# Two pieces instead of three for the turned maxima, queued reciprocals, and a re-ordered last stretch in an attention and token-mixer kernel

## The chip, the cores and the metric

The kernel runs on one core of one Trainium2 chip. The metric is the device time of one execution in microseconds (us). Before the change three runs took 1679.13 to 1680.25 us, with a median of 1679.38 us. The profiled execution is one more run: 1679.48 us, of which the profile covers a span of 1677.7 us.

## The reference

The input x has 2048 tokens of 512 channels. Two branches read its normalised rows. Cut to what matters:

```python
xn = layernorm(x)
# A: softmax attention, 32 heads of 16 channels
q, k, v = split(xn @ wqkv)
o = softmax(q @ k.T * 16 ** -0.5) @ v          # per head, 2048 x 2048 scores
s = o @ wo
# B: an MLP over the token axis, F = 1792
h = layernorm(xn)
u = gelu(einsum("bsd,sf->bdf", h, w1) + b1)
y = einsum("bdf,fs->bds", u, w2) + b2
out = x + s * silu(y.transpose())
```

All is float32. Products are made from values split into an upper part and a remainder (`three`: three matmuls for one product).

## The kernel before, in words

**The order is written out by hand.** The program is a list of instructions that each engine works off in its own order; no scheduler moves anything. Python loops over steps `s` in twos ("a pair"), from 0 to `total` = 534. `NU` = 512 is the number of half-blocks of maxima; `LEAD` = 22 is how many steps the maxima run ahead of the scores.

**One pair of the long middle part** (steps 22 to 510) holds, for two heads that sit in the two halves of TensorE's rows:

- 8 matmuls `mx` (line 393) of scores whose row maximum alone is wanted. VectorE reduces each one from PSUM (line 397, `mxp`). The pool `ps_mx` has three banks, so the fourth `mx` waits for the first reduction.
- 8 matmuls `sc` (line 771) of the scores that are used; ScalarE takes their exponentials (line 776, `prob`).
- two bursts of values, `values` (line 787, `av`), each of four matmuls that accumulate numerator and denominator of the softmax.
- up to 12 half matmuls of the token mixer (line 938, `dn`).

The strings in `ORDERS`, `ENDS` and `BEGINS` set the order of these within a pair, and the two numbers behind them (`places`) say in front of which entry the two bursts stand. At each place `piece()` is called, then the burst, then `run_later()`, which runs work that was put off by `after(n, f)` for n such calls.

**The maxima's sets.** After every 8 pairs, 16 half-blocks of maxima are complete (`max_rows`). They are reduced once more and negated on VectorE (line 412, `neg`), turned in four 32 x 32 blocks by VectorE (line 409, `f`), split by GpSimd (line 420, `m`) and written by four DMAs of GpSimd's queue as two extra rows of q. So the later score matmul subtracts the maximum by itself. `max_rows` returns these steps as functions; they go to the list `pieces`, and `piece()` runs one of them. There are 32 sets, 30 of them with both places of their pair in the middle part.

**Reciprocals.** For each group `g` of heads and each half `span` of the queries, `invert` takes the reciprocal of the denominators `d` (line 555, VectorE) and stores them (`rec_d`). There are eight. `divisions` later loads them and multiplies; `divide` puts its product on GpSimd while `now[0] < NU` and on VectorE afterwards (`eng`). The last of the six-head groups, span 1, gates the sixteen blocks of output products in `rest` (`until`).

**The last part.** From step 512 no maxima are left: a pair is 8 scores, two bursts and two calls of `take`, each of which takes one block of output products (line 897), as far as one is allowed. `own` handles the last pair of heads without a round trip through memory: turn with TensorE (`one`, line 629), reciprocal (632), a copy that spreads it (633), turn back (`two`, line 641), then `chunk`: multiply (647), upper part on ScalarE (648), remainder (79). For span 0 this runs between scores. For span 1 it runs at the very end, in four chunks of 128 columns, and 24 last matmuls (lines 86 to 88), eight multiplications by the gate (1093), eight additions (1097; four on GpSimd, four on VectorE) and eight stores follow.

Of the kernel before, what the change touches and what calls it, by code (L numbers as in the profile page):

```python
# [21 lines left out]
def tile_attention_token_mixer(ctx, tc, x, wqkv, wo, w1, b1, w2, b2, out):  # L22
    nc = tc.nc
    P = 128
# [339 lines left out]
    el = pool("el", 2, reuse_waits="tile")  # L364

    later = []
    now = [0]
# [31 lines left out]
    def max_rows(u):  # L399
# [17 lines left out]
        def last():  # L417
            turned(3)
            m = sm.tile([16, 2, P], F32R, name="m", bufs=1)
# [9 lines left out]

        return first_, lambda: turned(1, 2), last  # L430

# [117 lines left out]
    def invert(g, span):  # L549

        n = heads_of(g)
        d = dens[span][: DH * n, :]

        def two():
            nc.vector.reciprocal(d, d)
            nc.sync.dma_start(rec_d[g][span][:n, :].rearrange("h (j q) -> (h j) q", j=16), d)
            away.add((g, span))

        after(8 if g < ND - 1 else 4, two)

# [59 lines left out]
    def own(span, ev):  # L620
        rq = sm.tile([P, 4, 4], F32, name="rq", bufs=1)
        wide = el.tile([P, 512], F32, name="t", bufs=4)

        def one(pl=ps_mx, nm="mx"):

# [5 lines left out]
            for a in range(2):  # L631
                nc.vector.reciprocal(rq[:, :, 2 * a : 2 * a + 2], turned[:, :, 2 * a : 2 * a + 2, 16 - 16 * a])
            nc.vector.tensor_copy(
                wide.rearrange("p (k j r) -> p k j r", k=4, j=4), rq.unsqueeze(3).to_broadcast([P, 4, 4, 32]),
            )

        def two(pl=ps_mx, nm="mx"):

            ps = pl.tile([P, 512], F32, name=nm)
            for k in range(4):  # L640
                nc.tensor.matmul(
# [3 lines left out]

        def chunk(ps, of, at):
            nc.vector.tensor_tensor(out=ev[:, at], in0=ps[:, at], in1=ev[:, at], op=OP.mult)
            nc.scalar.copy(of[:, 0, at], ev[:, at])
            sub(nc.vector, of[:, 1, at], ev[:, at], of[:, 0, at])

        if span == QH - 1:
            asides.extend((one, two, chunk))
            return

        def move_in():
            ps = two()
            of = el.tile([P, 2, 512], F32R, name="uo")
            chunk(ps, of, slice(0, 512))
            for a in range(2):
# [314 lines left out]
    first_maxima = []  # L974
    pieces = []

# [7 lines left out]
    for s in range(0, total + 1, 2):  # L984
# [9 lines left out]
        if s < NU and t >= 0:  # L994
# [7 lines left out]
            for i, kinds in enumerate((*zip(first, second), "")):  # L1002
                if i in places:

                    piece()
                    now[0] = s + places.index(i)
# [48 lines left out]
        if s < NU and s % 16 == 14:  # L1055
            pieces.extend(max_rows(s + 1))
        while t < 0 and piece():
# [13 lines left out]
    run_later()  # L1071
    one, two, chunk = asides
# [5 lines left out]
    for k in range(4):  # L1078
        chunk(ps, of, slice(k * P, (k + 1) * P))
# [5 lines left out]
    banks = [(ps_sc, "sc"), (ps_mx, "mx"), (ps_sc, "sc"), (ps_mx, "mx"), (ps_sc, "sc"), (ps_av, "av"), (ps_mx, "mx"), (ps_dn, "dn")]  # L1085
    half = [NB // 2 + 4 * c + k for k in range(4) for c in range(2)]
    for n, b in enumerate(half):
        pl, nm = banks[n]
        po = pl.tile([P, 512], F32, name=nm)[:, :D]
# [3 lines left out]
        nc.vector.tensor_tensor(out=gates[b], in0=po, in1=gates[b], op=OP.mult)  # L1093

    for eng, some in ((nc.gpsimd, half[:4]), (nc.vector, half[4:])):
        for b in some:
            eng.tensor_tensor(out=gates[b], in0=ys[b], in1=gates[b], op=OP.add)
            nc.sync.dma_start(out[b * P : (b + 1) * P, :], gates[b])

# [26 lines left out]
```

## Time and profile before

| what | us |
|---|---|
| median of three runs | 1679.38 |
| profiled execution | 1679.48 |
| its span | 1677.7 |
| TensorE busy | 1654.7 (99%) |
| VectorE busy | 1424.5 (85%) |
| ScalarE busy | 1200.3 (72%) |
| GpSimd busy | 574.8 (34%) |

The profile of the execution counts from the start of the span. PE is TensorE, PEld its weight loads, DVE is VectorE, ACT ScalarE, POOL GpSimd, and SPq the queue that issues most DMAs. Matmul ends are modelled, so a PE that is shown busy can still be late: whether it is held up is read from when a burst of values comes round again. In a timeline, each row has the start, the length, the engine, the line, the operation, `out<-in`, shapes and a count; in brackets stands how long the engine was idle before it, and what ended that.

### The profile page before, as it was taken

To read this page: it belongs to the slowest core of one execution; us is meant where nothing else is said; L and a number is where in the kernel's file an instruction comes from. 1 tells how busy PE (TensorE), PEld (TensorE's weight loads), DVE (VectorE), ACT (ScalarE), POOL (GpSimd) and SP (SyncE) were. 2 spreads that over 40 slices of the span, in tenths; PEclk is the share of its full clock that TensorE was granted. 3 is DMA by queue.
4 is the path that set the end of the run, shared out by engine and by line. 5 is a ranking of instruction groups with operands and counts; after the bars stand their busy time and mean duration, and the time that the engine had idled before them with its cause. 6 is when DMAs were issued, how large, how long until landed. Compare 5 with 4: busy or idle time off the path is not lost.

```text
span 1677.7 us, 30703 instructions
## 1 busy us (share of the span) xinstructions
PE 1654.7 (99%) x11700; PEld 870.6 (52%) x11700; DVE 1424.5 (85%) x2476; ACT 1200.3 (72%) x2295; POOL 574.8 (34%) x674
## 2 busy tenths in 40 slices
PE   7999999999999999999999999999999999999997
PEld 6887644554454545544454444455454444444443
DVE  6655988888988989889898989899898998899945
ACT  3333277777777777777877777777777778888874
POOL 3223853332344332342322322222223222642321
PEclk9999999999999999999999999999999999999999
DMA  6568621505132141916141613123142515363345
GB/s 213 186 233 201 120 73 46 88 24 92 40 67 65 46 64 37 246 55 106 35 83 33 100 49 49 52 53 67 35 69 62 84 36 93 118 125 101 116 144 197
DMA packets 152175, 155.30 MB, mean 93 GB/s; under 512 B 51596, under 2 KB 109964, under 8 KB 148956
## 3 DMA queue, kind: packets, MB, share of 16 engines
q1 hardware_dynamic: 147612, 152.59, 37.8%
q8 instruction: 92, 1.51, 0.4%
q0 software_dynamic: 4416, 0.75, 0.4%
q14 instruction: 55, 0.45, 0.1%
HBM read 101.86 MB, written 50.32 MB: 91 GB/s over the span
## 4 chain that ended last, share of the span: by engine, by line
PE 96%; DVE 1%; DMA 1%; ACT 0%; issue 0%; SPq 0%; POOL 0%; DVEq 0%; POOLq 0%
PE av L787 30%; PE dn L938 23%; PE mx L393 17%; PE sc L771 14%; PE dn L897 3%; PE mx L303 2%; PE sc L303 2%; DVE mxp L397 1%; PE av L897 1%; PE dn L303 1%; PE av L303 1%; PE sc L86 0%; PE sc L87 0%; PE sc L88 0%; PE mx L771 0%; DMA gt<-g_d 0%
## 5 line engine op out<-in xcount | busy, mean ns | idle before, releaser
L397 DVE TENSOR_REDUCE mxp<-mx 128x1 f32<-128x512 f32 x2004 | 1243.4, 682 | 147.8 <-PE mx L393 97.3
L776 ACT ACTIVATE prob<-sc 128x512 f32<-128x512 f32 x2004 | 1050.5, 603 | 300.1 <-PE sc L771 200.1
L771 PE MATMUL sc<-big 50*128 50x512 f32 x2004 | 756.0, 418 | 0.6
L393 PE MATMUL mx<-big 48*128 48x512 f32 x2004 | 744.5, 421 | 0.7
L787 PE MATMUL av<-prob,vp 128*32 128x512 f32 x4096 | 545.6, 605 | 0.0
L938 PE MATMUL dn<-hu,wh 64*128 64x512 f32 x1556 | 538.7, 406 | 0.0
L393 PEld LDWEIGHTS mx<-big 48*128 48x128 f32 x2004 | 358.6, 185 | 284.6 <-DVE mxp L397 261.9
L771 PEld LDWEIGHTS sc<-big 50*128 50x128 f32 x2004 | 358.5, 185 | 100.9 <-ACT prob L776 82.5
L938 PE MATMUL dn<-hu,wl 64*128 64x512 f32 x778 | 316.8, 407 | 0.0
L938 PEld LDWEIGHTS dn<-hu,wh 64*128 64x128 f32 x1556 | 284.4, 184 | 45.1 <-issue 23.8
L938 PEld LDWEIGHTS dn<-hu,wl 64*128 64x128 f32 x778 | 143.5, 184 | 107.5 <-issue 79.7
L787 PEld LDWEIGHTS av<-prob,vp 128*32 128x32 f32 x4096 | 80.9, 108 | 177.5 <-issue 166.3
L79 POOL TENSOR_TENSOR wl<-raw,wh 128x512 fp32r<-128x512 f32 x124 | 150.8, 1219 | 38.9 <-ACT wh L150 30.3
L148 POOL CAST wh<-raw 128x512 fp32r<-128x512 f32 (+1 forms) x107 | 62.3, 582 | 268.9 <-PE dn L938 171.7
L420 POOL CAST m<-f 16x128 fp32r<-16x128 f32 x32 | 9.0, 281 | 279.3 <-DVE f L409 279.3
L479 POOL TENSOR_TENSOR sq<-u 128x512 f32<-128x512 f32 x14 | 14.6, 1043 | 179.1 <-ACT u L478 179.1
L83 POOL DMA_DIRECT2D big<-m x128 | 68.0, 538 | 0.0
L938 PE MATMUL dn<-wh,hu 64*128 64x512 f32 x156 | 55.4, 408 | 0.0
L515 POOL TENSOR_SCALAR t<-t 128x512 f32<-128x512 f32 x16 | 23.9, 1491 | 80.0 <-ACT t L512 80.0
L79 POOL TENSOR_TENSOR hu<-hx,hu 128x512 fp32r<-128x512 f32 x16 | 20.4, 1294 | 57.1 <-ACT hu L246 57.1
L776 ACT ACTIVATE prob<-mx 128x512 f32<-128x512 f32 x44 | 27.3, 620 | 14.0 <-PE sc L771 8.8
L303 PE MATMUL mx<-xt,big 128*128 128x512 f32 x144 | 35.3, 394 | 0.0
(200 smaller groups left out, 1125.7 us busy)
## 6 DMA issues: line engine op xcount, KB each, us to landing
raw<-in_B_w_dram SPq DMA_DIRECT2D x104, 256.0 KB
big<-k_d SPq DMA_DIRECT2D x96, 128.0 KB
big<-q_d SPq DMA_DIRECT2D x96, 128.0 KB
q_d<-sg SPq DMA_DIRECT2D x16, 512.0 KB
k_d<-sg SPq DMA_DIRECT2D x16, 512.0 KB
num_d<-ev SPq DMA_DIRECT2D x30, 256.0 KB
u_d<-uo SPq DMA_DIRECT2D x14, 512.0 KB
hu<-u_d SPq DMA_DIRECT2D x14, 512.0 KB
```

The costliest lines, as they stand in the source:

```text
L79: eng.tensor_tensor(out=o, in0=a, in1=b.bitcast(F32), op=OP.subtract)
L83: queue.dma_start(dst.bitcast(F32), src.bitcast(F32))
L148: nc.gpsimd.tensor_copy(whs[n][:, :m, :], raws[n][:, :m, :])
L303: nc.tensor.matmul(ps, w[part][:, kd, m], xt[kd][:, z, :], start=w is wh and z == 0 and kd == 0, stop=w is wl and kd == ND - 1,)
L393: nc.tensor.matmul(ps, q[o : o + 48, r * P : (r + 1) * P], k[o : o + 48, c * 512 : (c + 1) * 512], start=True, stop=True,)
L397: nc.vector.tensor_reduce(mxp[u // 16][:, a, r % 8, c : c + 1], ps, axis=AX.X, op=OP.max)
L515: nc.gpsimd.tensor_scalar(t, t, 1.0, None, op0=OP.add)
L771: nc.tensor.matmul(ps, ks[p][o : o + 50, kb * P : (kb + 1) * P], qs[p][o : o + 50, at : at + 512], start=True, stop=True,)
L776: nc.scalar.activation(e, ps, AF.Exp, scale=scale)
L787: nc.tensor.matmul(av[32 * j : 32 * j + 32, :], vps[p][:, kb, 16 * a : 16 * a + 32], prob.pop((t, a, c)), start=kb == 0, stop=kb == NB - 1,)
L897: nc.tensor.matmul(ps, w(slice(0, P)), m(slice(0, P)), start=first, stop=last)
L938: made.append(lambda r=r, start=first and a == lead, stop=last and a != lead: nc.tensor.matmul(ps, w(r), m(r), start=start, stop=stop,))
```

## The change

1. `max_rows` returns two functions and not three: the second turns blocks 1, 2 and 3.
2. `piece()` is called at the first place of a pair only.
3. A reciprocal of `invert` is no longer run by `run_later`: when its time has come it goes to the end of `pieces`. A new set of maxima goes to the front of that list.
4. The last stretch: the copy that spreads the reciprocals is made in four parts, the turn back goes to four banks, `chunk` is cut into `times` and `lower` so that a remainder stands behind the next chunk's multiplication, matmuls are issued before any multiplication by the gate, banks are taken in another order, and GpSimd adds three blocks instead of four.

```diff
         def last():
-            turned(3)
+            turned(1, 2, 3)
...
-        return first_, lambda: turned(1, 2), last
+        return first_, last
...
-        after(8 if g < ND - 1 else 4, two)
+        after(8 if g < ND - 1 else 4, lambda: pieces.append(two))
...
-            nc.vector.tensor_copy(
-                wide.rearrange("p (k j r) -> p k j r", k=4, j=4), rq.unsqueeze(3).to_broadcast([P, 4, 4, 32]),
-            )
+            for k in range(0, 4, 4 // spread):
+                nc.vector.tensor_copy(
+                    wide.rearrange("p (k j r) -> p k j r", k=4, j=4)[:, k : k + 4 // spread],
+                    rq[:, k : k + 4 // spread].unsqueeze(3).to_broadcast([P, 4 // spread, 4, 32]),
+                )
...
-        def chunk(ps, of, at):
+        def times(ps, of, at):
             nc.vector.tensor_tensor(out=ev[:, at], in0=ps[:, at], in1=ev[:, at], op=OP.mult)
             nc.scalar.copy(of[:, 0, at], ev[:, at])
+
+        def lower(of, at):
             sub(nc.vector, of[:, 1, at], ev[:, at], of[:, 0, at])
...
-                    piece()
+                    if i == places[0]:
+                        piece()
...
-            pieces.extend(max_rows(s + 1))
+            pieces[:0] = max_rows(s + 1)
...
-    one(ps_sc, "sc")
+    one, two, times, lower = asides
+    one(ps_sc, "sc", 4)
     take(3, whole)
-    ps = two()
+    shares = [two(pl, nm, [k]) for k, (pl, nm) in enumerate([(ps_sc, "sc"), (ps_mx, "mx")] * 2)]
...
+    for k in range(5):
+        if k < 4:
+            times(shares[k], of, cols[k])
+        if k > 0:
+            lower(of, cols[k - 1])
+            for n in (2 * k - 2, 2 * k - 1):
+                product(n)
+
+    for n in range(8):
+        gated(n)
+        if n < 3:
+            added(n, nc.gpsimd)
+    for n in range(3, 8):
+        added(n, nc.vector)
```

What this does to the order on the engines is seen at three places. A row is a line, an operation, `out<-in` with the program's names, the size of the output and a count.

**VectorE, one set of maxima of the middle part with a reciprocal behind it.** `mxp` are the row maxima of one matmul, `neg_...` the set's negated maxima, `f` their turned form, `d` the denominators. Before:

```order
L412 TENSOR_REDUCE neg_130<-mxp 128x16
L409 STREAM_TRANSPOSE f<-neg_130 32x32
L397 TENSOR_REDUCE mxp<-mx 128x1 x3
L409 STREAM_TRANSPOSE f<-neg_130 32x32 x2
L397 TENSOR_REDUCE mxp<-mx 128x1 x5
L409 STREAM_TRANSPOSE f<-neg_130 32x32
L397 TENSOR_REDUCE mxp<-mx 128x1 x51
L555 RECIPROCAL d<-d 128x64
L397 TENSOR_REDUCE mxp<-mx 128x1 x5
```

After (the lines have moved: 409 is 410, 397 is 398, 412 is 413, 555 is 556):

```order
L413 TENSOR_REDUCE neg_130<-mxp 128x16
L410 STREAM_TRANSPOSE f<-neg_130 32x32
L398 TENSOR_REDUCE mxp<-mx 128x1 x8
L410 STREAM_TRANSPOSE f<-neg_130 32x32 x3
L398 TENSOR_REDUCE mxp<-mx 128x1 x8
L556 RECIPROCAL d<-d 128x64
L398 TENSOR_REDUCE mxp<-mx 128x1 x48
```

The two turns that stood after three reductions of the set's pair now stand one place further on, with the last one; a reciprocal no longer stands five reductions ahead of a set's end, but at the first place of the second pair behind a set.

**TensorE, the end of the wait for the last divided group, around step 512.** Matmuls of lines 771 and 777 are scores, 787 and 793 values, 897 and 903 the output products. Before:

```order
L787 MATMUL av<-prob,vp 32x512 x4
L771 MATMUL mx<-big 128x512
L771 MATMUL sc<-big 128x512
L771 MATMUL mx<-big 128x512
L771 MATMUL sc<-big 128x512
L771 MATMUL mx<-big 128x512
L771 MATMUL sc<-big 128x512
L787 MATMUL av<-prob,vp 32x512 x4
L897 MATMUL dn<-wh,hu 128x512
```

After, behind the same burst and the same six scores:

```order
L793 MATMUL av<-prob,vp 32x512 x4
L777 MATMUL mx<-big 128x512
L777 MATMUL sc<-big 128x512
L793 MATMUL av<-prob,vp 32x512 x4
L777 MATMUL mx<-big 128x512
L777 MATMUL sc<-big 128x512
L777 MATMUL mx<-big 128x512
L777 MATMUL sc<-big 128x512
L777 MATMUL mx<-big 128x512
L777 MATMUL sc<-big 128x512
L793 MATMUL av<-prob,vp 32x512 x4
L903 MATMUL dn<-wh,hu 128x512
```

One more pair goes by without output products, and all sixteen blocks come later by it. In exchange the half pair without one, which stood behind the seventh and eighth block (the wait for `own_done`), is gone, and so is one of the three at the end.

**VectorE, the last stretch.** `rq` are the reciprocals of the last pair of heads, `t` their spread form, `ev` numerators, `big` behind line 79 the remainder. Before:

```order
L633 COPY t<-rq 128x512
L647 TENSOR_TENSOR ev<-mx,ev 128x128
L79 TENSOR_TENSOR big<-ev,big 128x128
L647 TENSOR_TENSOR ev<-mx,ev 128x128
L79 TENSOR_TENSOR big<-ev,big 128x128
```

After:

```order
L635 COPY t<-rq 128x128 x4
L650 TENSOR_TENSOR ev<-sc,ev 128x128
L650 TENSOR_TENSOR ev<-mx,ev 128x128
L79 TENSOR_TENSOR big<-ev,big 128x128
L650 TENSOR_TENSOR ev<-sc,ev 128x128
L79 TENSOR_TENSOR big<-ev,big 128x128
```

The copy is in four parts, and each remainder stands behind the next multiplication. Behind these, on VectorE, stand eight multiplications by the gate as before, and then five additions in place of four.

More of the change, by code (lines that the diff above doesn't have):

```diff
@@ L364, in tile_attention_token_mixer @@
     el = pool("el", 2, reuse_waits="tile")
+    pieces = []
     later = []
@@ L622, in own, with one @@
         wide = el.tile([P, 512], F32, name="t", bufs=4)
-        def one(pl=ps_mx, nm="mx"):
+        def one(pl=ps_mx, nm="mx", spread=1):
             ps = pl.tile([P, 512], F32, name=nm)
@@ L632, in one, with two @@
                 nc.vector.reciprocal(rq[:, :, 2 * a : 2 * a + 2], turned[:, :, 2 * a : 2 * a + 2, 16 - 16 * a])
-            nc.vector.tensor_copy(
-                wide.rearrange("p (k j r) -> p k j r", k=4, j=4), rq.unsqueeze(3).to_broadcast([P, 4, 4, 32]),
-            )
-        def two(pl=ps_mx, nm="mx"):
+            for k in range(0, 4, 4 // spread):
[3 more added lines that the diff above has]
+                )
+        def two(pl=ps_mx, nm="mx", ks=range(4)):
             ps = pl.tile([P, 512], F32, name=nm)
-            for k in range(4):
+            for k in ks:
                 nc.tensor.matmul(
@@ L644, in two @@
             return ps
-        def chunk(ps, of, at):
+        def times(ps, of, at):
             nc.vector.tensor_tensor(out=ev[:, at], in0=ps[:, at], in1=ev[:, at], op=OP.mult)
             nc.scalar.copy(of[:, 0, at], ev[:, at])
+        def lower(of, at):
             sub(nc.vector, of[:, 1, at], ev[:, at], of[:, 0, at])
         if span == QH - 1:
-            asides.extend((one, two, chunk))
+            asides.extend((one, two, times, lower))
             return
@@ L657, in move_in @@
             of = el.tile([P, 2, 512], F32R, name="uo")
-            chunk(ps, of, slice(0, 512))
+            times(ps, of, slice(0, 512))
+            lower(of, slice(0, 512))
             for a in range(2):
@@ L1071, in tile_attention_token_mixer @@
     run_later()
-    one, two, chunk = asides
-    one(ps_sc, "sc")
+    one, two, times, lower = asides
+    one(ps_sc, "sc", 4)
     take(3, whole)
-    ps = two()
+    shares = [two(pl, nm, [k]) for k, (pl, nm) in enumerate([(ps_sc, "sc"), (ps_mx, "mx")] * 2)]
     of = ks[NP - 1][:, :1024].rearrange("p (a q) -> p a q", a=2)
     left = []
-    for k in range(4):
-        chunk(ps, of, slice(k * P, (k + 1) * P))
     while open_ or later or soon:
@@ L1084, in tile_attention_token_mixer, with product @@
         f()
-    banks = [(ps_sc, "sc"), (ps_mx, "mx"), (ps_sc, "sc"), (ps_mx, "mx"), (ps_sc, "sc"), (ps_av, "av"), (ps_mx, "mx"), (ps_dn, "dn")]
+    banks = [(ps_sc, "sc"), (ps_mx, "mx"), (ps_sc, "sc"), (ps_mx, "mx"), (ps_av, "av"), (ps_dn, "dn"), (ps_sc, "sc"), (ps_mx, "mx")]
     half = [NB // 2 + 4 * c + k for k in range(4) for c in range(2)]
-    for n, b in enumerate(half):
-        pl, nm = banks[n]
-        po = pl.tile([P, 512], F32, name=nm)[:, :D]
+    sums = {}
+    def product(n):
+        b, (pl, nm) = half[n], banks[n]
+        po = sums[b] = pl.tile([P, 512], F32, name=nm)[:, :D]
         at = slice(n // 2 * P, (n // 2 + 1) * P)
@@ L1092, in tile_attention_token_mixer, with gated, added @@
         three(po, of[:, 0, at], of[:, 1, at], w[:, 0, :], w[:, 1, :], True, True)
[L1093 to L1098, printed above, removed]
+    def gated(n):
+        b = half[n]
+        nc.vector.tensor_tensor(out=gates[b], in0=sums[b], in1=gates[b], op=OP.mult)
+    def added(n, eng):
+        b = half[n]
+        eng.tensor_tensor(out=gates[b], in0=ys[b], in1=gates[b], op=OP.add)
+        nc.sync.dma_start(out[b * P : (b + 1) * P, :], gates[b])
+    cols = [slice(k * P, (k + 1) * P) for k in range(4)]
+    for k in range(5):
[11 more added lines that the diff above has]
+        added(n, nc.vector)
 _INS = ["A_x", "A_wqkv", "A_wo", "B_w1", "B_b1", "B_w2", "B_b2"]
```

1 line of the change is left out of this document (removed).

## The prediction

> **What bounds the kernel now.** I read the page first (busy time, then the groups), then timelines of VectorE and of the bursts of values in the middle part, then the end.
>
> ```profile
> PE 1654.7 (99%) x11700; PEld 870.6 (52%) x11700; DVE 1424.5 (85%) x2476; ACT 1200.3 (72%) x2295; POOL 574.8 (34%) x674
> L397 DVE TENSOR_REDUCE mxp<-mx 128x1 f32<-128x512 f32 x2004 | 1243.4, 682 | 147.8 <-PE mx L393 97.3
> L393 PEld LDWEIGHTS mx<-big 48*128 48x128 f32 x2004 | 358.6, 185 | 284.6 <-DVE mxp L397 261.9
> ```
>
> TensorE looks full, but its weight loads for `mx` wait for a reduction to free a bank. Most of that waiting lies behind bursts and costs nothing; the question is where VectorE makes the burst itself come late. In the middle part a burst of values (line 787) opens each pair; here is a pair without a set (1005.12), the pair with a set's first two pieces (1010.80), the next with its third (1016.81), and one without:
>
> ```profile
> 1005.12 1.06 PE L787 MATMUL av<-prob,vp 128*32 128x512 f32 x8
> ...
> 1010.80 1.07 PE L787 MATMUL av<-prob,vp 128*32 128x512 f32 x8
> ...
> 1016.81 1.06 PE L787 MATMUL av<-prob,vp 128*32 128x512 f32 x8
> ...
> 1022.48 1.07 PE L787 MATMUL av<-prob,vp 128*32 128x512 f32 x8
> ```
>
> From first burst to first burst: 5.68, 6.01, 5.67 us. So a set costs 0.33 us, all of it in the pair that has two places with pieces. VectorE over the same stretch:
>
> ```profile
> 1006.92 4.96 DVE L397 TENSOR_REDUCE mxp<-mx 128x1 f32<-128x512 f32 x8 [0.73 <-PE mx L393]
> 1011.91 0.22 DVE L412 TENSOR_REDUCE neg<-mxp 128x16 f32<-128x64 f32 x1
> 1012.24 0.20 DVE L409 STREAM_TRANSPOSE f<-neg 32x32 f32<-32x32 f32 x1
> 1012.59 1.89 DVE L397 TENSOR_REDUCE mxp<-mx 128x1 f32<-128x512 f32 x3 [0.15 <-PE mx L393]
> 1014.51 0.41 DVE L409 STREAM_TRANSPOSE f<-neg 32x32 f32<-32x32 f32 x2
> 1014.86 3.02 DVE L397 TENSOR_REDUCE mxp<-mx 128x1 f32<-128x512 f32 x5
> 1017.92 0.20 DVE L409 STREAM_TRANSPOSE f<-neg 32x32 f32<-32x32 f32 x1
> 1018.60 4.95 DVE L397 TENSOR_REDUCE mxp<-mx 128x1 f32<-128x512 f32 x8 [0.48 <-PE mx L393]
> ```
>
> What to see: in a plain pair VectorE has one hole of 0.73 us, under the first burst, and eight reductions in a row otherwise (4.96 us). The first piece (0.22 and 0.20 us) filled that hole and the next reduction still found its matmul just ready (0.15 us idle), so it cost nothing. The two turns of 0.41 us stood in front of five reductions without a hole, and TensorE waited for banks. The single turn left 0.48 us of the hole unused.
>
> **The change part by part.** *Sets.* The second place is freed: 0.33 us for this set. The first and the last of the 30 sets with both places in this part, each as the distance of two opening bursts:
>
> ```profile
> 238.21 1.07 PE L787 MATMUL av<-prob,vp 128*32 128x512 f32 x8
> ...
> 244.22 1.07 PE L787 MATMUL av<-prob,vp 128*32 128x512 f32 x8
> ...
> 1551.75 1.06 PE L787 MATMUL av<-prob,vp 128*32 128x512 f32 x8
> ...
> 1557.36 1.06 PE L787 MATMUL av<-prob,vp 128*32 128x512 f32 x8
> ```
>
> 6.01 us against 5.68 for a pair of that make, and 5.61 against 5.44 for the shorter late pairs. Taken so for all 30 against pairs of the same make, 24 lose 0.3 to 0.4 us, the last three 0.28, 0.26 and 0.16, and three irregular ones 0 to 0.1: 8.9 us in all. The two turns come into the hole of the next pair: 3 turns in place of 1 are 0.20 + 0.41 = 0.61 us, and the hole is 0.73. They are hidden there by the burst of 1.06 us. GpSimd's `m` and its DMAs wait for them: 0.4 us later behind the burst, 0.33 us earlier in all, so nothing is late next.
>
> *Reciprocals.* All eight move from a second place to a first place, behind both pieces of a set.
>
> ```profile
> L409 DVE STREAM_TRANSPOSE f<-neg 32x32 f32<-32x32 f32 x128 | 25.6, 200 | 6.0 <-DVE neg L412 0.5
> L412 DVE TENSOR_REDUCE neg<-mxp 128x16 f32<-128x64 f32 x32 | 7.0, 218 | 0.8
> L555 DVE RECIPROCAL d<-d 128x64 f32<-128x64 f32 x6 | 3.3, 554 | 0.2
> ...
> 914.18 1.07 PE L787 MATMUL av<-prob,vp 128*32 128x512 f32 x8
> 920.31 1.06 PE L787 MATMUL av<-prob,vp 128*32 128x512 f32 x8
> 917.90 0.55 DVE L555 RECIPROCAL d<-d 128x64 f32<-128x64 f32 x1
> ```
>
> This pair took 6.13 us, 0.45 more than 5.68. Four of the eight lose that, the others 0.40, 0.20, 0.27 and 0.28: 2.9 us. At the first place 0.55 us fits the 0.73. The store `rec_d` goes behind one more load on SP's queue; its readers load a pair later and are not waited for until the last part. The instructions that VectorE runs are as many as before.
>
> *What does not fit.* The nine or so late and irregular pairs have no such hole. At the end of the middle part:
>
> ```profile
> 1473.01 2.48 DVE L397 TENSOR_REDUCE mxp<-mx 128x1 f32<-128x512 f32 x4 [0.15 <-PE sc L771]
> 1475.75 0.69 DVE L397 TENSOR_REDUCE mxp<-mx 128x1 f32<-128x512 f32 x1 [0.26 <-PE mx L393]
> ```
>
> Holes of 0.15 and 0.26 us there, 0.41 together, for 0.41 us of turns or 0.55 of a reciprocal: between 0 and 0.14 us lost where both holes serve, up to 0.33 (the old price) where none does. I take 0.08 for each of nine: 0.7 us; bounds 0 and 3.
>
> *The last blocks.* The last reciprocal comes a pair later, and with it all output products. A pair more runs without them, and there ScalarE, with eight exponentials, is the longer one:
>
> ```profile
> 1595.31 0.59 ACT L776 ACTIVATE prob<-mx 128x512 f32<-128x512 f32 x1
> ...
> 1597.70 0.65 ACT L776 ACTIVATE prob<-sc 128x512 f32<-128x512 f32 x1
> ...
> 1628.89 1.06 PE L787 MATMUL av<-prob,vp 128*32 128x512 f32 x8
> 1630.31 1.06 PE L787 MATMUL av<-prob,vp 128*32 128x512 f32 x8
> 1632.10 0.47 PE L897 MATMUL dn<-wh,hu 128*128 128x512 f32 x1 [0.73 <-DMA hu<-uo]
> ```
>
> Five exponentials start in 2.39 us, so eight take 3.82. Two half pairs without products vanish, one behind the eighth block and one at the end, each as the one between 1628.89 and 1630.31: 1.42 us; and the wait of 0.73 us for the moved rows `hu` goes, since the first block that needs them now comes three half pairs behind the turn back, and not two. 3.82 - 2.84 - 0.73 = +0.25 us, say +0.3. Bounds: -0.7 if TensorE hides ScalarE's lag in its six banks, +1.5 if the gates' loads, which queue on SP behind the last blocks' stores, come late.
>
> *The last stretch.* Four copies of 128 columns, four returns to four banks, and interleaved chunks:
>
> ```profile
> 1661.10 1.16 PE L641 MATMUL mx<-ident,t 128*128 128x128 f32 x8 [0.83 <-DVE t L633]
> 1662.36 0.29 DVE L647 TENSOR_TENSOR ev<-mx,ev 128x128 f32<-128x128 f32 x1 [1.32 <-PE mx L641]
> 1663.04 0.69 PE L86 MATMUL sc<-uo,big 128*128 128x512 f32 x1 [0.79 <-ACT big L648]
> 1665.81 0.68 DVE L1093 TENSOR_TENSOR prob<-sc,prob 128x512 f32<-128x512 f32 x1
> 1670.44 0.69 DVE L1093 TENSOR_TENSOR prob<-dn,prob 128x512 f32<-128x512 f32 x1
> 1671.04 2.98 DVE L1097 TENSOR_TENSOR prob<-big,prob 128x512 f32<-128x512 f32 x4
> ...
> 1671.04 1.18 DVE L1097 TENSOR_TENSOR prob<-big,prob 128x512 f32<-128x512 f32 x1
> ...
> 1664.00:1666.00 2.00, 2.00 (x6) 1.61 (x5) 1.27 (x6) 0.60 (x2) 0.00 (x0) 0.50 0.22 85
> ```
>
> The first multiplication waited 1.32 us for the whole return. Now it waits for a quarter of it (0.29 us of 1.16) and for four small copies, of which I take 0.21 us each (a 128-column operation of 0.29 us less the overlap seen between such operations): it starts near 1661.45 on the old time axis, 0.9 us earlier, and so does the first of the 24 last matmuls (1662.13). The last multiplication by the gate stands 7.40 us behind the first matmul (1670.44 - 1663.04) and moves along: TensorE feeds it. Then five additions: the first of four took 1.18 us beside GpSimd's last one, the other three 0.60 each. GpSimd will be done with three by then, so 5 x 0.60 = 3.0, as long as 2.98 before. The end is 0.9 us earlier. Bounds: the last row is a stretch of 2 us in which TensorE's granted clock was 0.50. About a third of the 24 matmuls ran so, which makes 7.40 / 32 = 0.23 us for one at full clock. If all ran at full clock, VectorE's chain would bind (eight times 0.69 us from the last remainder, near 1663.7), and 0.8 us more be won: -1.7. If twice as many ran at half clock, 8 x 0.2 = 1.6 us would be lost: +0.7.
>
> The Trainium skill ("TensorE: Matmul & The Clock Gate", Part 1: The HAM clock gate) says that a free-running window of some 3.4 us decides the clock from activity, so that where the slow stretch falls depends on its phase. By that rule the half clock may fall on fewer matmuls or on more, and the trace agrees so far as one such stretch stands behind the idle time before 1663.04: by the rule this term is anywhere between those bounds, by the rows as they lie -0.9.
>
> **Sum.** -8.9 - 2.9 + 0.7 + 0.3 - 0.9 = -11.7 us. Against the profiled execution (1679.48 us: its span of 1677.7 and 1.8 around it; the median is 0.1 lower) that gives 1667.8 us.
>
> **The rivals.**
> - *The turns overflow.* Three turns in a row, or their hand-over to the reduction behind, need 0.9 us or more and the stall returns in the next pair at some 0.2 us. For it: 0.15 us passed between the first piece's turn and the next reduction. Against it: that reduction waited for its matmul, and the two turns passed in 0.41. 30 x 0.2 in place of 0.7: 1673.1 us.
> - *The late blocks hold up the end.* The extra pair is not paid back, because the chain of stores and loads for the last blocks delays the gates: +3 us more, 1670.8 us.
> - *The change doesn't do what it says:* the 0.33 us belong to TensorE's order in that pair and not to VectorE. Against it: the same order in the next pairs gives 5.67 us. 1679 us.
> - *Slower.* A first place that must first drain the reductions before it, and then delays the matmul of the first reduction: with three turns the pair behind a set would have to lose more than 11.8 / 30 = 0.39 us net, from a piece of 0.73 + 0.39 = 1.1 us and up; at 0.6 us lost, 1686 us. The single turn that stands there now (5.67 us) speaks against it.
> - *More is won:* irregular waits near the change of matrices go as well, or the last matmuls run at full clock throughout: 1665 us.
>
> **How the numbers follow.** Forecast 0.73, with its own range of 1665.5 to 1670; overflow 0.10; late blocks 0.06; no effect 0.03; slower 0.02; more won 0.06. The range 1664.8 to 1671.5 leaves out overflow and the two behind it, 0.15, and a little of the rest. A measurement of this kernel tells 0.2% (3.4 us) from no change: faster 0.95, same 0.03, slower 0.02.
>
> **What would show it.** Right: opening bursts 5.68 us apart in a set's pair and in the next, three turns within 0.65 us followed by a reduction without a late burst, a reciprocal alone under a first burst; the last burst of the kernel some 11 us earlier in the span; the first last matmul 3.2 us behind the end of the last burst and not 4.1. Wrong: 5.9 us in the pair behind a set; loads of gates that the first multiplication waits for; half clock over more than ten of the 24 matmuls.

## The result and the profile after

The changed kernel took 1667.77 us (median of 6 runs, 1666.13 to 1668.87), and the kernel before, on the same chip, 1679.72 (median of 6, 1679.13 to 1680.25): a ratio of 0.9927, 95% interval 0.9917 to 0.9937, 11.95 us less. The forecast was 1667.8 us, within 1664.8 to 1671.5. The profiled execution took 1667.68 us, with a span of 1665.9.

To see where the time went, the span is cut at three opening bursts of values: the first of all, that of step 508 and the very last (this one from its first weight load). All times are us; the runs below the first two rows are the experiments that follow.

| kernel | start | middle | last blocks | end | span |
|---|---|---|---|---|---|
| before | 215.26 | 1369.76 | 71.85 | 20.80 | 1677.7 |
| changed | 216.40 | 1359.66 | 71.33 | 18.48 | 1665.9 |
| after_again | 216.02 | 1360.17 | 71.40 | 19.06 | 1666.7 |
| sets_only | 215.15 | 1361.90 | 71.66 | 20.74 | 1669.5 |
| recips_only | 215.28 | 1367.78 | 71.36 | 20.76 | 1675.2 |
| tail_only | 215.21 | 1369.35 | 72.05 | 18.41 | 1675.0 |
| late_even_gates | 215.91 | 1358.86 | 71.24 | 18.58 | 1664.6 |
| second_place | 214.21 | 1389.62 | 71.36 | 19.48 | 1694.7 |
| one_piece | 215.06 | 1367.37 | 72.30 | 18.60 | 1673.3 |
| r3_old | 214.61 | 1359.84 | 71.56 | 18.41 | 1664.4 |
| copy_whole | 215.38 | 1359.54 | 71.11 | 19.28 | 1665.3 |
| chunks_in_turn | 214.96 | 1359.56 | 71.41 | 19.54 | 1665.5 |
| four_adds | 216.17 | 1359.54 | 71.45 | 18.61 | 1665.8 |

Changed against before: +1.14, -10.10, -0.52, -2.32, together -11.8 us. The start scatters between 214.2 and 216.4 us over these thirteen profiles, and where the edits in it are the same (changed, after_again, sets_only, r3_old) still between 214.6 and 216.4. So single times a us apart tell nothing; parts of the span do. The middle scatters less: 0.4 us between before and tail_only, whose middles are the same program, and 0.6 us among the five profiles with the changed kernel's middle (changed, after_again, copy_whole, chunks_in_turn, four_adds). The last blocks of these five lie between 71.1 and 71.5 us. Why the end differs between kernels with the same last stretch (18.41 to 19.48 us) is told under "The end".

The page of the changed kernel, the rows that answer to the first three of before:

```profile
PE 1644.1 (99%) x11700; PEld 871.3 (52%) x11700; DVE 1426.0 (86%) x2482; ACT 1194.2 (72%) x2295; POOL 569.9 (34%) x671
L398 DVE TENSOR_REDUCE mxp<-mx 128x1 f32<-128x512 f32 x2004 | 1244.6, 684 | 134.9 <-PE mx L394 93.8
L394 PEld LDWEIGHTS mx<-big 48*128 48x128 f32 x2004 | 358.6, 185 | 270.6 <-DVE mxp L398 248.7
```

VectorE does as much as before (1426.0 us against 1424.5), and TensorE still looks 99% busy. The weight loads waited for a reduction 248.7 us instead of 261.9. That is 13 us less, of the size of the gain, and VectorE was idle in front of its reductions 12.9 us less (134.9 against 147.8); these two rows are the only ones shown here that point at the cause. The timeline of TensorE, its opening bursts at the set that the prediction showed (a pair opens with every second burst):

```profile
1000.46 1.06 PE L793 MATMUL av<-prob,vp 128*32 128x512 f32 x8
...
1006.14 1.07 PE L793 MATMUL av<-prob,vp 128*32 128x512 f32 x8
...
1011.81 1.06 PE L793 MATMUL av<-prob,vp 128*32 128x512 f32 x8
...
1017.48 1.07 PE L793 MATMUL av<-prob,vp 128*32 128x512 f32 x8
```

and VectorE over the same stretch:

```profile
1002.25 4.95 DVE L398 TENSOR_REDUCE mxp<-mx 128x1 f32<-128x512 f32 x8 [0.71 <-PE mx L394]
1007.12 0.21 DVE L413 TENSOR_REDUCE neg<-mxp 128x16 f32<-128x64 f32 x1
1007.43 0.20 DVE L410 STREAM_TRANSPOSE f<-neg 32x32 f32<-32x32 f32 x1
1007.93 4.95 DVE L398 TENSOR_REDUCE mxp<-mx 128x1 f32<-128x512 f32 x8 [0.30 <-PE mx L394]
1012.91 0.63 DVE L410 STREAM_TRANSPOSE f<-neg 32x32 f32<-32x32 f32 x3
1013.61 4.95 DVE L398 TENSOR_REDUCE mxp<-mx 128x1 f32<-128x512 f32 x8
```

The pair without a set, the set's pair and the next are 5.68, 5.67 and 5.67 us apart, where the set's pair took 6.01. The three turns take 0.63 us between two groups of eight reductions, VectorE has no more than 0.1 us of idle time left there, and the next opening burst comes on time. The end of the changed kernel, a timeline of all engines, and below it a row of a table of stretches (length, busy time of PE, PEld, DVE, ACT and POOL with counts, granted clock, DMA share, GB/s):

```profile
1651.13 0.63 DVE L635 COPY t<-rq 128x128 f32<-128x128 f32 x4
...
1652.68 0.51 PE L86 MATMUL sc<-uo,big 128*128 128x512 f32 x1
...
1654.13 0.68 DVE L1103 TENSOR_TENSOR prob<-sc,prob 128x512 f32<-128x512 f32 x1
...
1654.96 3.80 POOL L1107 TENSOR_TENSOR prob<-big,prob 128x512 f32<-128x512 f32 x3 [57.72 <-DVE prob L1103]
1654.99 0.69 DVE L1103 TENSOR_TENSOR prob<-mx,prob 128x512 f32<-128x512 f32 x1 [0.18 <-DMA prob<-g_d]
...
1658.58 0.68 DVE L1103 TENSOR_TENSOR prob<-mx,prob 128x512 f32<-128x512 f32 x1
1659.18 3.10 DVE L1107 TENSOR_TENSOR prob<-big,prob 128x512 f32<-128x512 f32 x5
...
1652.70:1658.50 5.80, 5.77 (x24) 4.41 (x24) 5.52 (x13) 0.73 (x3) 3.54 (x3) 1.00 0.71 269
```

The last burst ends at 1649.43, so the first of the 24 last matmuls (1652.68) stands 3.25 us behind it; 3.2 was forecast. The granted clock is 1.00 over all 24 matmuls. From the first of them to the last multiplication by the gate are 5.90 us, not 7.40.

### The profile page after: what moved, and what is told of

The parts are those of the page before. It is cut to its first block, busy times and chain, and to the rows that moved or that the text cites. A ratio compares the mean times of both kernels' runs of the same rounds, so it can differ in the third digit from the quotient of the medians.

```text
span 1665.9 us, 30703 instructions
## 1 busy us (share of the span) xinstructions
PE 1644.1 (99%) x11700; PEld 871.3 (52%) x11700; DVE 1426.0 (86%) x2482; ACT 1194.2 (72%) x2295; POOL 569.9 (34%) x671
## 4 chain that ended last, share of the span: by engine, by line
PE 96%; DVE 2%; DMA 1%; ACT 1%; issue 0%; POOL 0%; SPq 0%; DVEq 0%; POOLq 0%
PE av L793 30%; PE dn L944 23%; PE mx L394 17%; PE sc L777 13%; PE dn L903 3%; PE mx L303 2%; PE sc L303 2%; DVE mxp L398 1%; PE av L903 1%; PE dn L303 1%; PE av L303 1%; ACT prob L782 1%; PE mx L777 0%; PE sc L86 0%; PE sc L88 0%; PE sc L87 0%
## 5 line engine op out<-in xcount | busy, mean ns | idle before, releaser
L398 DVE TENSOR_REDUCE mxp<-mx 128x1 f32<-128x512 f32 x2004 | 1244.6, 684 | 134.9 <-PE mx L394 93.8
L394 PEld LDWEIGHTS mx<-big 48*128 48x128 f32 x2004 | 358.6, 185 | 270.6 <-DVE mxp L398 248.7
L782 ACT ACTIVATE prob<-mx 128x512 f32<-128x512 f32 x44 | 28.1, 639 | 13.7 <-PE sc L777 13.6
```

Source lines behind the costliest of these rows:

```text
L394: nc.tensor.matmul(ps, q[o : o + 48, r * P : (r + 1) * P], k[o : o + 48, c * 512 : (c + 1) * 512], start=True, stop=True,)
L398: nc.vector.tensor_reduce(mxp[u // 16][:, a, r % 8, c : c + 1], ps, axis=AX.X, op=OP.max)
L782: nc.scalar.activation(e, ps, AF.Exp, scale=scale)
```

## The experiments

The theory was the prediction's: VectorE has 0.73 us under the first burst of a pair and nothing elsewhere, so what stands there is free up to that size. The rivals were that the place doesn't matter and only the number of pieces does, and that anything fits at a first place. For the end the question was what bound it: TensorE (as predicted), VectorE, or GpSimd.

### One part at a time

sets_only: the two functions of `max_rows` and the call at the first place, and nothing else of the change.

```diff
-            turned(3)
+            turned(1, 2, 3)
...
-        return first_, lambda: turned(1, 2), last
+        return first_, last
...
-                    piece()
+                    if i == places[0]:
+                        piece()
```

> Only parts 1 and 2 of the change: sets of maxima in two pieces, one piece a pair at the first place; reciprocals and last stretch as before. Stages: start (to the first burst of values), middle (from there to the burst of step 508), last blocks (to the last burst), end. Before: 215.3, 1369.8, 71.9, 20.8 us. Theory (VectorE's hole under the first burst hides the pieces): middle shorter by the 8.9 us of the 30 sets, less 0.43 in the pair of step 146 and 3 x 0.23 in the pairs behind the last three sets, as the changed kernel shows them: -7.8, 1362.0; the other stages as before; time some 1672 us. Rival (the 0.33 us belong to the order of matmuls or come back elsewhere without the moved reciprocals): middle within 3 us of 1369.8.

Measured: 1671.29 us, ratio 0.9951 (0.9937 to 0.9966); middle -7.86, end -0.06. The theory's -7.8 came; the rival, a middle within 3 us of before, did not.

recips_only: sets as before, but reciprocals at the first place of a pair in which no piece stands.

```diff
-        after(8 if g < ND - 1 else 4, two)
+        after(8 if g < ND - 1 else 4, lambda: turns.append(two))
...
-                    piece()
+                    if not piece() and i == places[0] and turns:
+                        turns.pop(0)()
```

> Only part 3: the eight reciprocals wait in a list of their own and run at the first place of a pair in which no piece of a set is due; sets in three pieces at both places and the last stretch as before. Theory: 2.9 us off the eight pairs that had them, +0.44 in the pair of step 164, whose first place has no hole, and +0.5 near step 502, where a copy to the upper part lands beside two other ScalarE copies: middle 1369.8 - 2.0 = 1367.8; last blocks 0.5 us shorter; end 20.8; time some 1677 us. Rival (reciprocals were hidden already and what the changed kernel won in their pairs came from the sets): middle 1369.8.

Measured: 1677.22 us, ratio 0.9988 (0.9978 to 0.9997); middle -1.98, last blocks -0.49. The four pairs that lost 0.45 lose nothing now (5.67 and 5.68 us).

tail_only: the new last stretch (part 4 of the change) with everything else as before.

> Only part 4: the last stretch of the changed kernel, sets and reciprocals as before. Theory A (the 2.3 us at the end come from order, and full clock follows from it, since TensorE idles less): end 18.5 us with no half clock over the last 24 matmuls; other stages as before. Theory B (where the half clock falls depends on a phase that has nothing to do with the kernel): 18.5 with full clock, 19.9 with a stretch at half clock, and either can come. Time 1677.4 or 1678.8.

Measured: 1677.01 us, ratio 0.9985 (0.9975 to 0.9994); end -2.39, at a granted clock of 1.00 over the 24 matmuls. Both theories allow that, so it doesn't choose between them. But sets_only and recips_only, which keep the old end, show no half clock over these matmuls either, so full clock doesn't come from the new order alone.

after_again: the changed kernel once more, run beside these three.

> The changed kernel once more, as a control: middle 1359.7, last blocks 71.3. The start was 1.1 us longer in the changed kernel's profile than in the one before though nothing is changed there: if that is chance it differs now by up to 1 us. Theory A on the end: 18.5 us and full clock again; theory B: may show a half clock and up to 19.9.

Measured: 1667.68 us, ratio 0.9929 (0.9914 to 0.9944). By parts of the span the three edits add up: the middle -7.86 - 1.98 = -9.84 against -10.10 for the whole, the end -2.39 against -2.32. The medians of the three add up to 13.2 us and the whole to 11.9; a scatter like that of the start is as large as this difference, and it was not followed further. The end of after_again is 0.58 us longer than that of the changed kernel, from the same program.

### The place and the size of a piece

second_place: the changed kernel with its pieces at the other place of the pair.

```diff
-                    if i == places[0]:
+                    if i == places[1]:
```

> The changed kernel, its pieces unchanged (one turn, then three; reciprocals behind them) but run at the second place of each pair instead of the first. Theory (the place decides: the hole of 0.73 us lies under the first burst only): a set's pair grows by about 0.4 us and the next by about 0.55, 0.98 in all for some 28 sets, and a reciprocal costs 0.45 again: the middle part goes from 1359.7 to some 1387 to 1390 us, the time to about 1696. Rival (fewer, longer pieces were the gain, the place is indifferent): middle 1359.7 to 1361, time 1668 to 1669.

Measured: 1696.44 us in one run, middle 1389.62: 30 us more than the changed kernel, with the same instructions on VectorE. Its opening bursts at the set shown above, and VectorE at the second of these pairs:

```profile
1022.14 1.07 PE L793 MATMUL av<-prob,vp 128*32 128x512 f32 x8
...
1028.13 1.07 PE L793 MATMUL av<-prob,vp 128*32 128x512 f32 x8
...
1034.36 1.06 PE L793 MATMUL av<-prob,vp 128*32 128x512 f32 x8
```

```profile
1029.93 1.89 DVE L398 TENSOR_REDUCE mxp<-mx 128x1 f32<-128x512 f32 x3 [0.73 <-PE mx L394]
1031.85 0.63 DVE L410 STREAM_TRANSPOSE f<-neg 32x32 f32<-32x32 f32 x3
1032.41 3.02 DVE L398 TENSOR_REDUCE mxp<-mx 128x1 f32<-128x512 f32 x5
```

The pairs take 5.99 and 6.23 us here, and 6.12 and 6.24 at most other sets: 0.45 and 0.56 lost. The hole of 0.73 us stands unused in front of the three reductions at 1029.93, 1.9 us ahead of the turns; time that VectorE idles there is not given back later in the pair. The theory's numbers came (middle 1387 to 1390), and the rival's did not.

one_piece: a whole set at one first place.

```diff
-        return first_, last
+        return (lambda: (first_(), last()),)
```

> The changed kernel with each set in one piece: the negation, all four turns and what follows stand at one first place. Theory (the hole has a size): the piece takes about 1.2 us of VectorE against a hole of 0.73, so 0.35 to 0.45 us are lost in each of some 28 sets, about what the old second place cost: middle 1369 to 1372 us, time about 1679. Rival (a first place hides whatever stands there, since the bank queue of the maxima refills behind it): middle 1359.7, time 1668.

Measured: 1675.10 us in one run, middle 1367.37, 7.7 us more than the changed kernel. TensorE's opening bursts and VectorE at a regular set:

```profile
1054.37 1.06 PE L793 MATMUL av<-prob,vp 128*32 128x512 f32 x8
...
1060.34 1.07 PE L793 MATMUL av<-prob,vp 128*32 128x512 f32 x8
```

```profile
1055.49 0.22 DVE L413 TENSOR_REDUCE neg<-mxp 128x16 f32<-128x64 f32 x1
1055.81 0.84 DVE L410 STREAM_TRANSPOSE f<-neg 32x32 f32<-32x32 f32 x4
1056.59 4.82 DVE L398 TENSOR_REDUCE mxp<-mx 128x1 f32<-128x512 f32 x8
```

From 1055.49 to the end of the turns at 1056.65 are 1.16 us, and such a pair takes 5.93 to 5.97 us, 0.25 to 0.29 more than a plain one (at four of the sets, where the negation starts 0.08 us ahead of the last reduction's end, it takes 5.81 to 5.84). So a first place takes about 0.88 us without loss. That is the hole of 0.73 and some 0.13 more: the eight reductions behind the piece take 4.82 us, and those of the changed kernel, shown above, 4.95, so VectorE makes up a part of its lag within the pair. The loss that I expected (0.35 to 0.45; middle 1369 to 1372) left this out. The rival, that everything fits, falls.

### The late pairs

In the changed kernel six pairs are longer than before: those of steps 146 (+0.43), 164 (+0.45), 466 (+0.24), 482 (+0.22), 498 (+0.25) and 502 (+0.48), 2.1 us together. VectorE at step 146, whose pair opens at 562.63:

```profile
562.26 1.89 DVE L398 TENSOR_REDUCE mxp<-mx 128x1 f32<-128x512 f32 x3 [0.24 <-PE mx L394]
564.18 0.63 DVE L410 STREAM_TRANSPOSE f<-neg 32x32 f32<-32x32 f32 x3
564.75 2.43 DVE L398 TENSOR_REDUCE mxp<-mx 128x1 f32<-128x512 f32 x4
```

Its first place lies so early in the pair that the burst gives VectorE no hole at all: the turns stand between reductions, as at a second place. That this costs the 0.43 us is read from these rows. In second_place the pair takes 6.56 us where it takes 6.77 here, so for this pair the first place is the worse of the two.

r3_old: the changed kernel with the last two reciprocals run by `run_later`, as before.

```diff
-        after(8 if g < ND - 1 else 4, lambda: pieces.append(two))
+        after(8, lambda: pieces.append(two)) if g < ND - 1 else after(4, two)
```

> The changed kernel with the last two reciprocals (those that the last blocks wait for) run by their due time as before the change. Theory: the last blocks begin their output products a pair earlier, and that brings nothing back or costs: last blocks 71.7 to 71.9 us instead of 71.3, the wait for the moved rows hu (0.73 us) is there again; the pair of step 502 goes from 5.94 to 5.46 and two pairs lose 0.28 each again, middle 1359.6 to 1360. Rival (the later start of the products costs TensorE a pair without cover, as the prediction had it): last blocks 0.3 us shorter than in the changed kernel, 71.0.

Measured: 1666.18 us in one run; the pair of step 502 takes 5.44 us again (-0.50), those of 490 and 506 lose 0.28 and 0.29 again, and the last blocks take 71.56 (theory 71.7 to 71.9, rival 71.0, so nearer to the theory). ScalarE shows why step 502 is linked to a reciprocal ten steps earlier. The changed kernel, and then r3_old (the pairs open at 1559.20 and 1557.79):

```profile
1562.17 0.61 ACT L713 COPY t<-dn 128x512 f32<-128x512 f32 x1
1563.07 0.59 ACT L528 COPY ev<-av 128x512 f32<-128x512 f32 x1 [0.28 <-PE av L793]
1563.55 0.62 ACT L602 CAST hu<-u 96x512 fp32r<-96x512 f32 x1
1564.07 2.04 ACT L782 ACTIVATE prob<-sc 128x512 f32<-128x512 f32 x4
```

```profile
1558.60 0.67 ACT L602 CAST hu<-sq 96x512 fp32r<-96x512 f32 x1
...
1560.76 0.61 ACT L713 COPY t<-dn 128x512 f32<-128x512 f32 x1
1561.66 0.59 ACT L528 COPY ev<-av 128x512 f32<-128x512 f32 x1 [0.28 <-PE av L793]
1562.14 2.20 ACT L782 ACTIVATE prob<-sc 128x512 f32<-128x512 f32 x4
```

The divided rows `hu` come a pair later with their reciprocal, and their upper part then falls behind two other copies on ScalarE, ahead of four exponentials. These start 4.87 us into the pair instead of 4.35.

late_even_gates: late sets in two and two turns, no reciprocal at an early first place, the last group's first reciprocal as before (the expectation calls it the last of all; the edit moves the last but one, back to step 490), and the last gates loaded in the order of their use.

```diff
+        at_first = 2 if u > 456 else 1
...
-            turned(0)
+            turned(*range(at_first))
...
-            turned(1, 2, 3)
+            turned(*range(at_first, 4))
...
-        after(8 if g < ND - 1 else 4, lambda: pieces.append(two))
+        after(8 if g < ND - 1 else 4, two if (g, span) == (ND - 1, 0) else lambda: pieces.append(two))
...
+    order_of_use = [NB // 2 + 4 * c + k for k in range(4) for c in range(2)]
...
-        for b in range(lo, hi):
+        for b in order_of_use[lo - NB // 2 : hi - NB // 2]:
...
-                    if i == places[0]:
+                    if i == places[0] and not (places[0] == 1 and pieces and pieces[0].__name__ == "two"):
```

> The changed kernel with three edits where its traces showed loss: the late sets (from step 457 on) are split into two and two turns instead of one and three; a reciprocal is not run at a first place that lies early in its pair (there no burst covers it), and the last reciprocal of all is run by its due time as before the change; the gates of the last stretch are loaded in the order in which they are used. Theory (late pairs lose because the piece is longer than their small holes): the pairs of steps 466, 482 and 498 go from 5.68 to about 5.45 us, the pair of step 164 from 6.68 to about 6.23, the pair of step 502 from 5.94 to 5.46 with 0.28 given back where the reciprocal stands; middle 1358.5 instead of 1359.7; the second multiplication by a gate no longer waits for its load (0.2 to 0.8 us of the end): in all 1666.3 us against 1667.7. Rival (those pairs are long for another reason, ScalarE's copies or the matrices' change): middle 1359.7 and time within 0.5 us of the changed kernel.

Measured: 1665.56 us (median of 5, 1664.74 to 1666.70), ratio to before 0.9919 (0.9905 to 0.9932); middle 1358.86. Pair by pair against the changed kernel: 164 -0.44, 466 and 482 -0.15 each, 498 -0.23, 502 -0.50, 490 +0.30; others within 0.05. The pairs of 466 and 482 were expected at 5.45 us and took 5.53. The late pairs do lose by VectorE's pieces, and the pair of 502 by ScalarE. The wait for the second gate is gone, but the end part is 18.58 us against 18.48: the last multiplication by the gate starts only 0.08 us earlier behind the last burst (11.12 us against 11.20), since now the last three start 0.68 us apart, held by their matmuls, and the ones ahead 0.60; and from the last addition to the end of the span are 3.76 us and not 3.59, which stays open. So 0.9 us of the gain are shown in the middle and the last blocks; that its median is 2.2 us below the changed kernel's is more than these show, and the two ratios' intervals overlap.

### The end

sets_only keeps the old end and shows it without the half clock: a row of its table of stretches, then VectorE's and GpSimd's additions.

```profile
1656.00:1664.00 8.00, 4.65 (x21) 3.49 (x19) 7.27 (x15) 0.60 (x2) 4.99 (x4) 1.00 0.32 120
```

```profile
1658.48 4.99 POOL L1098 TENSOR_TENSOR prob<-big,prob 128x512 f32<-128x512 f32 x4 [57.77 <-DVE prob L1094]
...
1662.43 1.58 DVE L1098 TENSOR_TENSOR prob<-big,prob 128x512 f32<-128x512 f32 x1
```

At full clock its last multiplication by the gate starts 13.1 us behind the last burst, 13.6 in the profile of before, and yet the end part is 20.74 us against 20.80. GpSimd's fourth addition ends at 1663.47, and VectorE's first one, issued at 1662.43, ends 0.54 behind that, at 1664.01. In the profile of before the fourth ends at 1671.68 and VectorE's first at 1672.22, again 0.54 behind. So the old end hung on GpSimd: its first addition starts 9.8 us behind the last burst in both.

The Trainium skill ("SBUF — State Buffer", Who interferes with whom) says that a VectorE instruction with two inputs in SBUF contends with a GpSimd instruction that reads SBUF, and that the ports they share are an exclusive lock. The traces agree: VectorE's multiplications by the gate, which have one input in PSUM, run 0.60 us apart beside GpSimd, and an addition of two SBUF tiles takes 1.18 or 1.58 us beside it and 0.68 alone.

What the end of the changed kernel still waits for is a load. Its second multiplication by the gate waits 0.18 us for its gate, in after_again 0.75 and in second_place 1.17, and their end parts are 18.48, 19.06 and 19.48 us. In tail_only and r3_old it doesn't wait, and the end part is 18.41 in both. The loads are issued on SP's queue right behind the last blocks' last store (issued at 1647.78 and 1655.47 in the two kernels shown); first the changed kernel, whose last burst opens at 1647.39, then tail_only (1656.62):

```profile
1648.21 4.17 SPq L765 DMA_DIRECT2D prob<-g_d  x8
```

```profile
1655.91 4.61 SPq L764 DMA_DIRECT2D prob<-g_d  x8
```

The first is issued 0.8 us behind the opening of the last burst and not 0.7 ahead of it, as in each kernel whose very last reciprocal waits in the list (recips_only too, where the old order's later multiplications hide it), and in none where it doesn't. The late gates that the prediction named in a bound of the last blocks so came in part, and they came in the end part.

copy_whole: the copy and the return undivided.

```diff
-    one(ps_sc, "sc", 4)
+    one(ps_sc, "sc")
...
-    shares = [two(pl, nm, [k]) for k, (pl, nm) in enumerate([(ps_sc, "sc"), (ps_mx, "mx")] * 2)]
+    shares = [two()] * 4
```

> The changed kernel, in its last stretch the copy of the reciprocals undivided (one of 512 columns) and the return through one bank, as before the change; chunks still divided in turns, GpSimd still adding three. Theory (VectorE's chain behind the first chunk binds, and it starts as late as the return): the first of the 24 last matmuls some 0.7 to 0.9 us later, the end part 19.2 us instead of 18.45. Rival (the chunks' order or GpSimd's additions bind the end): end part 18.4 to 18.6.

```profile
1649.77 0.43 DVE L635 COPY t<-rq 128x512 f32<-128x512 f32 x1
1651.52 0.49 DVE L650 TENSOR_TENSOR ev<-mx,ev 128x128 f32<-128x128 f32 x2 [1.32 <-PE mx L644]
```

Measured: end part 19.28 us, +0.80 (+0.87 against tail_only and r3_old, which wait for no gate, as this run). From the start of the copy to the first multiplication are 1.75 us, against 0.88 in the changed kernel (1651.13 to 1652.01 there).

chunks_in_turn: each chunk's remainder right behind its multiplication.

```diff
-    for k in range(5):
-        if k < 4:
-            times(shares[k], of, cols[k])
-        if k > 0:
-            lower(of, cols[k - 1])
-            for n in (2 * k - 2, 2 * k - 1):
-                product(n)
+    for k in range(4):
+        times(shares[k], of, cols[k])
+        lower(of, cols[k])
+    for n in range(8):
+        product(n)
```

> The changed kernel with each chunk's remainder right behind its own multiplication on VectorE, as before the change, and all products behind the fourth chunk in the program. Theory (VectorE waits for ScalarE's rounding in each chunk, some 0.3 to 0.45 us four times, before it comes to the gates): the first multiplication by a gate 1.2 to 1.6 us later and the end part 19.6 to 20.0 us instead of 18.45. Rival (TensorE feeds the gates, as the prediction had it, so VectorE's waits are hidden): end part below 18.9.

```profile
1651.20 0.29 DVE L79 TENSOR_TENSOR big<-ev,big 128x128 fp32r<-128x128 f32 x1 [0.36 <-ACT big L651]
...
1653.78 0.29 DVE L79 TENSOR_TENSOR big<-ev,big 128x128 fp32r<-128x128 f32 x1 [0.36 <-ACT big L651]
1653.99 0.68 DVE L1103 TENSOR_TENSOR prob<-sc,prob 128x512 f32<-128x512 f32 x1
```

Measured: end part 19.54 us, +1.06 (19.6 to 20.0 expected, below 18.9 by the rival). The first and the last of the 24 matmuls start as early as in the changed kernel (5.30 and 10.67 us behind the last burst, there 5.30 and 10.69), but the last multiplication by the gate starts at 12.24 and not at 11.20. So in this run VectorE binds, which waits for ScalarE 0.36 us in each of four chunks, and TensorE doesn't.

four_adds: GpSimd adds four blocks.

```diff
-        if n < 3:
+        if n < 4:
...
-    for n in range(3, 8):
+    for n in range(4, 8):
```

> The changed kernel with GpSimd adding four blocks and VectorE four. Theory (the old end was bound by GpSimd's fourth addition, since VectorE's first addition beside it is slow): GpSimd's fourth addition ends about 0.9 us behind VectorE's last gate, VectorE's first addition takes 1.2 to 1.5 us instead of 0.6, and the end part is 18.5 to 19.2 us, so none of the 0.6 us of the addition that VectorE gives away comes back. Rival (VectorE's additions alone set the end): one addition less, end part 17.9.

```profile
1654.74 5.03 POOL L1107 TENSOR_TENSOR prob<-big,prob 128x512 f32<-128x512 f32 x4 [57.87 <-DVE prob L1103]
...
1659.15 2.98 DVE L1107 TENSOR_TENSOR prob<-big,prob 128x512 f32<-128x512 f32 x4
```

Measured: end part 18.61 us against 18.48. VectorE's four additions take 2.98 us, the five of the changed kernel 3.10: its first takes 1.17 us while GpSimd's fourth lasts until 1659.77. Giving the fourth to VectorE is worth 0.1 to 0.2 us (18.41 where the second gate isn't waited for).

## Why the prediction was right, point by point

The total was right within 0.1 us; that is partly luck, since two terms were off by 1.4 us in opposite directions, a third by 0.8, and the start of that execution was 1.1 us longer for a reason that the runs don't show (r3_old, whose start is the same program, took 214.61 us for it).

- *Sets, -8.9.* Right. sets_only's middle is -7.86 with 1.1 us of overflow in the pairs of 146, 466, 482 and 498; without it -9.0. All regular sets' pairs take 5.66 to 5.69 us.
- *Reciprocals, -2.9.* Right in the same sense: -1.98, of which the pairs of 164 and 502 take back 0.9.
- *What does not fit, +0.7.* Mis-sized: 2.1 us, within the bounds of 0 and 3. I priced nine pairs at 0.08; six lost 0.22 to 0.48. The price took 0.41 us of turns, but the piece that comes there holds three, 0.61 us by the prediction's own sum. And two holes in a late pair don't serve one piece together: where no set is due, VectorE idles 0.31 us at the first place and 0.15 four reductions on (the pair of step 478 in the changed kernel); behind the three turns of step 466 the second hole still stands unused, 0.21 us. So 0.63 us of turns cost some 0.24. That the pairs of 146 and 164 have their first place where no burst covers it stands in the program's order, and I had not looked there. The pair of 502 was lost on ScalarE, an engine that this step did not name.
- *The last blocks, +0.3.* The sign was wrong (-0.52). The inserted pair without products took what was forecast, 3.82 us:

```profile
1588.43 1.06 PE L793 MATMUL av<-prob,vp 128*32 128x512 f32 x8
...
1590.86 1.07 PE L793 MATMUL av<-prob,vp 128*32 128x512 f32 x8
1592.28 1.06 PE L793 MATMUL av<-prob,vp 128*32 128x512 f32 x8
```

  These are TensorE's bursts in the changed kernel; the two half pairs from 1588.43 to 1592.28 are 3.85 us. The half pairs that vanish gave 1.42 and 1.90 us (the second was priced at 1.42 too), the wait for `hu` 0.77. What the step missed is a second wait near the end, here of before and then of the changed kernel:

```profile
1650.92 0.50 PE L897 MATMUL dn<-wh,hu 128*128 128x512 f32 x1 [0.71 <-DVE gt L747]
```

```profile
1642.87 0.50 PE L903 MATMUL dn<-wh,hu 128*128 128x512 f32 x1 [0.39 <-DVE gt L753]
```

  The half pair with the first of them takes 2.31 us instead of 3.10; the 0.39 lies in the next one, which takes 3.24 us instead of 2.78. So 3.85 - 1.42 - 1.90 - 0.77 - 0.79 + 0.46 = -0.57, and 0.05 of it is lost again in small changes. The reason given with the lower bound, that TensorE's banks would hide ScalarE's lag, is not what happened. The rival "late blocks hold up the end" failed at its price of 3 us; r3_old, without the inserted pair, has 71.56, so the insertion costs nothing in the last blocks. Its mechanism is there, though: the gates come late in the end part, by 0.18 us in the changed kernel and up to 1.17 in the others.
- *The last stretch, -0.9.* Mis-sized: -2.3, outside its bounds of -1.7 and +0.7. The start of the 24 matmuls moved as forecast, by 0.86 us (6.16 to 5.30 us behind the last burst; four small copies took 0.63 us and not 0.84). The step that failed is "TensorE feeds it", by which the last multiplication by the gate stays 7.40 us behind the first of these matmuls: it stands 5.90 behind. The old end hung on VectorE's late first multiplication by the gate and then on GpSimd's fourth addition, and neither on TensorE nor on its clock: undone one at a time, the divided copy is worth 0.80 us, the interleaved chunks 1.06 and the fourth addition 0.1, together 2.0 of the 2.3; the earlier issue of the matmuls and the other banks were not undone alone. TensorE feeds the last multiplications in the new end: in tail_only and r3_old the last two start 0.69 us apart, each behind its matmuls, and in the changed kernel VectorE is 0.1 us behind that. I had the row of 1.18 us beside GpSimd's last addition and did not ask who waited for whom there. The bound for a binding VectorE took 0.69 us for each of eight multiplications, their length; they start 0.60 us apart, and that alone is 0.7 us.

The half clock ran over some of the 24 matmuls in the profile of before alone. In the twelve others the stretch of half clock starts behind them. The clock gate's rule that I cited (the Trainium skill, "TensorE: Matmul & The Clock Gate", Part 1: The HAM clock gate) left open where that stretch falls. The traces agree that it can fall on the matmuls or behind them, and the measurement decides what it is worth here: nothing, 20.80 us with it and 20.74 without.

Of the rivals, "more is won" had one of its two sources right: the last matmuls ran at full clock throughout, but that was worth nothing to the old end (20.74 us with it), and the irregular pairs lost instead. "The turns overflow" named the right limit (0.9 us at a first place; one_piece shows 0.88) and the wrong piece, since three turns take 0.63. "Doesn't do what it says" and "slower" are ruled out by second_place, where the same pieces at the other place cost 30 us.

## What to carry to other kernels

Price a piece of work by the place where it stands on its engine, not by its length: here 0.63 us of turns cost nothing under a burst, 0.24 between short holes and 0.56 among back-to-back reductions. Read the place in the order of every irregular stretch, not only in the regular one, and follow each moved step to the engines that work on its result. In a last stretch, ask of the last operation on each engine who waited for it before pricing anything by TensorE; for a row of operations on one engine, use the distance of their starts and not their length.

## What the runs showed of the hardware

- A hole is lost if it isn't used at its moment: with 0.73 us idle 1.9 us ahead of a piece, the piece still cost its length less 0.07 us (0.56 of 0.63).
- An addition of 128x512 on VectorE took 0.68 us alone and up to 1.58 beside GpSimd's, ending 0.54 us behind GpSimd's end; GpSimd's took 1.25 to 1.30 in any case.
- Four copies of 128 columns took 0.63 us and one of 512 columns 0.43. So dividing it cost 0.2 us of VectorE and let the first multiplication start 0.87 us sooner.
